# Attention with 16 queries a head: K loaded in 64 KB rows through a ring of two transposed pieces

## The chip, the cores and the metric

One Trainium2 chip, one core. The metric is device time in microseconds (us) of one execution, lower is better. The median of the runs shown is 631.35 us (3 runs, 631.29 to 631.35).

## The reference

```python
B, H, Sq, Skv, Dh = 8, 16, 16, 2048, 256        # all bfloat16
scale = q.shape[-1] ** -0.5
scores = jnp.einsum('bhqd,bhkd->bhqk', q, k) * scale
attn = softmax(scores, axis=-1)
return jnp.einsum('bhqk,bhkd->bhqd', attn, v)
```

There are 128 heads (8 batches of 16), each with only 16 queries against 2048 keys. K and V are 128 MiB each and each byte is used once, so nearly all that the kernel does is to move K and V from memory.

## The kernel before

**Blocks.** The 128 heads are taken eight at a time, in G = 16 blocks. A block's K is 8 MiB and so is its V. Each lies in SBUF with 128 tokens ("t") on every partition, 256 numbers a token, so a partition's share is one row of 64 KB in memory. A partition holds tokens of one head only: sixteen partitions make a head. `SL` has four slots of 64 tokens a partition: `VA, VB` hold a block's V, `KA, KB` its K.

**Score products (QK), lines 296 and 297.** K has the tokens on the partitions, and the product wants the head dimension there. DVE therefore transposes K in blocks of 32x32 words, in place in its slot (`kt`, line 200, 128x4096 words an instruction, four a block). The queries are laid out as sparse weights `QW`, which ACT writes for each block (`qwb`, line 256) from `QT`, a copy of Q that POOL makes at the start (line 184). PE then makes 64 products of 512 columns a block into the four banks of `S_ps`, one weight load for two products.

**Softmax.** DVE takes the row maximum over `S_ps` (line 222), ACT the exponential into `P_sb` with its row sum (line 282), DVE two transposes of `P_sb`, into `PTa` and `PTb` (lines 226 and 227), and the reciprocal.

**Weights' copies (`copies`, lines 207, 209 and 269).** The transposed probabilities are copied into the sparse weight tile `PTz`, in two halves e = 0, 1 for tokens 0 to 63 and 64 to 127. Each half takes eight copies, two for each quarter r of the partitions. DVE makes those of e = 0, r = 2, 3; ACT the other twelve.

**Output products (PV), line 317.** 128 products a block, each with its own weight load, 256 columns, summed in `O_ps`. PV needs all eight copies of e = 0 and the V of the block; from token 64 on the copies of e = 1. ACT then scales `O_ps` into `O_all` (`evac`, line 262); for the last block DVE does (line 247).

**Order.** The order on each engine is written out by hand, with semaphores between the engines. PE's loop runs QK of block r, then 20 spare products whose result is not used (`SPARE` = 5 rounds of four into `X_ps`), then PV of block r - 1. DVE's loop, for block g: maximum, two transposes of P, first transpose of the next K, its four copies, the other three transposes of K.

**Transfers.** All are issued by SP on one queue, in a fixed order: Q, K0, K1, V0, K2, V1, K3, V2 and so on. K goes in two transfers of 64 tokens a block (rows of 32 KB), V from block 2 on in one of 128 tokens (rows of 64 KB), V of blocks 0 and 1 in two of 64. A K transfer waits until PE has used that slot, a V transfer until PV of the block before has read V. At the end K15 goes in four transfers, V14 in three pieces, V15 in eight, the last of five tokens, so that PV can follow closely:

```python
PIECES = {last - 1: [(0, 60), (60, 39), (99, 29)],
          last: [(0, 28), (28, 32), (60, 23), (83, 16), (99, 11), (110, 8), (118, 5), (123, 5)]}
```

A piece (a, n) of V15 is issued when PV14 has read tokens up to a + n, rounded up to 16 tokens. Behind V15 go the output of fifteen blocks and, last, that of block 15.

Of the kernel before, what the change touches and what calls it, by code (L numbers as in the profile page):

```python
# [10 lines left out]
SP = mybir.EngineType.SP  # L11
BF16 = mybir.dt.bfloat16
# [3 lines left out]
SPARE = 5  # L16
VA, VB, KA, KB = 0, 1, 2, 3
# [3 lines left out]
def bass_standalone__softmax_full_bidir__sampling_kernel(  # L21
# [16 lines left out]
    ku = k.rearrange("b h s d -> (b h s) d").rearrange("(u p t) d -> u p t d", p=128, t=T)  # L38
# [4 lines left out]
    with ExitStack() as es:  # L43
        ec = es.enter_context
        SL = ec(nc.sbuf_tensor("SL", [128, 4, T, D], BF16))
        QT = ec(nc.sbuf_tensor("QT", [128, SQ * D], BF16))
        QW = ec(nc.sbuf_tensor("QW", [128, 2, 128, 8], BF16))

        P_sb = ec(nc.sbuf_tensor("P_sb", [128, 2080], BF16))

        PTa = ec(nc.sbuf_tensor("PTa", [128, T, 32], BF16))
# [5 lines left out]
        O_all = ec(nc.sbuf_tensor("O_all", [128, G + 2, D], BF16))  # L57
# [5 lines left out]
        O_ps = ec(nc.psum_tensor("O_ps", [128, 512], F32))  # L63
        X_ps = ec(nc.psum_tensor("X_ps", [128, 512], F32))

        def sem(name):
# [3 lines left out]
        s_k0 = [sem("s_k0a"), sem("s_k0b")]  # L70
        s_k = [sem("s_ka"), sem("s_kb")]
        s_kl = [sem("s_kla"), sem("s_klb")]
        s_v = sem("s_v")
        s_v0 = sem("s_v0")
# [5 lines left out]
        c_k0 = sem("c_k0")  # L80
        c_kt = [sem("c_kt0"), sem("c_kt1")]
# [11 lines left out]
        SLf = SL[:].bitcast(F32)  # L93

        QX = PTz[:, 1, 0:SQ * D // 128, :].rearrange("p t m -> p (t m)")

        QXu = QX.rearrange("p (c u a y) -> p a u c y", u=8, a=4, y=2)

        QTu = QT[:].rearrange("p (c u y) -> p u c y", u=32, y=2)

        SLk = SL[:].rearrange("p s (c t) (b i q) -> p s c b q t i", t=16, i=32, q=2)


        PIECES = {last - 1: [(0, 60), (60, 39), (99, 29)],
                  last: [(0, 28), (28, 32), (60, 23), (83, 16), (99, 11), (110, 8), (118, 5), (123, 5)]}

        s_p = {a: sem("s_p%d" % a) for a in sorted({a for w in PIECES for a, n in PIECES[w][1:]})}
        VW = SL[:, VA:VB + 1, :, :].rearrange("p a t d -> p (a t) d")

# [10 lines left out]
        def qx(Q, a):  # L120

            return (QTu[32 * a:32 * a + 32, 8 * Q:8 * Q + 8, :, :].rearrange("p u c y -> p c u y"),
                    QXu[32 * Q:32 * Q + 32, a, :, :, :].rearrange("p u c y -> p c u y"))

        def load_k(eng, g, e, slot, t0, n, s):
            eng.dma_start(SL[:, slot, t0:t0 + n, :], ku[2 * g + e, :, t0:t0 + n, :]).then_inc(s, 16)  # L126

        def on_sync(eng):
            def load_v(w, a, n):

                eng.wait_ge(c_pv, 8 * w + (a + n + C - 1) // C)
                eng.dma_start(VW[:, a:a + n, :], vb[w, :, a:a + n, :]).then_inc(s_p[a] if a else s_v, 16)  # L132

            eng.dma_start(QX, qh).then_inc(s_q, 16)
            for g, s0, s in ((0, VA, s_k0), (1, KA, s_k)):
                for e in range(2):
                    load_k(eng, g, e, s0 + e, 0, T, s[e])

            for e in range(2):
                eng.wait_ge(c_qk, 4 * e + 4)  # L140
                eng.dma_start(VW[:, T * e:T * e + T, :], vb[0, :, T * e:T * e + T, :]).then_inc(s_v0 if e else s_v, 16)
            for e in range(2):
                eng.wait_ge(c_qk, 4 * e + 12)
                load_k(eng, 2, e, KA + e, 0, T, s_k[e])
            for e in range(2):
                eng.wait_ge(c_pv, 4 * e + 12)
                eng.dma_start(VW[:, T * e:T * e + T, :], vb[1, :, T * e:T * e + T, :]).then_inc(s_v0 if e else s_v, 16)
            with nc.Fori(3, last, engines=[SP], hint_back_edge=True) as j:
                for e in range(2):
                    eng.wait_ge(c_qk, 8 * j + 4 * e - 4)  # L150
                    load_k(eng, j, e, KA + e, 0, T, s_k[e])
                load_v(j - 1, 0, 2 * T)
            for e in range(2):
                eng.wait_ge(c_qk, 8 * last + 4 * e - 4)
                load_k(eng, last, e, KA + e, 0, T // 2, s_k[e])
                load_k(eng, last, e, KA + e, T // 2, T // 2, s_kl[e])
            for w in PIECES:
                for a, n in PIECES[w]:
                    load_v(w, a, n)
            eng.wait_ge(c_ev, G)  # L160
            eng.dma_start(oh[:, 0:last, :], O_all[:, 2:G + 1, :]).then_inc(s_st, 16)
            eng.wait_ge(c_ev, G + 1)
            eng.dma_start(oh[:, last, :], O_all[:, G + 1, :]).then_inc(s_st, 16)
            eng.wait_ge(s_st, 32)

        def on_gpsimd(eng):

            for x, n in ([(c_pv, 8)] + [(x, 1) for x in s_kl] +
                         [(s_p[a], 16 * G - 16 * sum(a in dict(PIECES[w]) for w in PIECES)) for a in s_p]):
                eng.sem_inc(x, n)  # L170
            eng.memset(QW[:].rearrange("p e m x -> p (e m x)").bitcast(F32), 0.0).then_inc(c_qt, 1)
# [3 lines left out]
            eng.memset(P_sb[:, 0:16], 0.0).then_inc(c_mk, 1)  # L175
            eng.memset(P_sb[:, 2064:2080], 0.0).then_inc(c_mk, 1)
            eng.wait_ge(c_mk, 3)
# [3 lines left out]
            for n in range(16):  # L181

                eng.wait_ge(c_cq if n else c_pool, max(n, 1))
                eng.tensor_copy(*qx(n // 4, n % 4)).then_inc(c_cq, 1)  # L184

            eng.wait_ge(c_qw, 4)
            eng.wait_ge(c_cq, 16)
            eng.wait_ge(c_mk, 7)
            eng.memset(zero[1], 0.0).then_inc(c_pool, 1)

        def on_vector(eng):
# [6 lines left out]
            def kt(e, h, slot, n=1, first=False):  # L198
                x = SLf[:, slot, 32 * h:32 * h + 32 * n, :].rearrange("p t i -> p (t i)")
                eng.transpose(x, x).then_inc(c_k0 if first else c_kt[e], n)  # L200
# [11 lines left out]
            for e in range(2):  # L212
                eng.wait_ge(s_k0[e], 16)
                for h in range(2):
                    kt(e, h, VA + e, 1, True)

            eng.wait_ge(s_k[0], 16)
            kt(0, 0, KA, 2)
            eng.wait_ge(c_pool, 2)
            with nc.Fori(0, G, engines=[DVE]) as g:  # L220
                eng.wait_ge(c_qk, 8 * g + 8)
                eng.tensor_reduce(out=negm[:], in_=S_ps[:].rearrange("p c n -> p (c n)"),  # L222
                                  axis=AX.X, op=ALU.max, negate=True).then_inc(c_mx, 1)
                eng.wait_ge(c_ex, g + 1)
                eng.wait_ge(c_co[1], 8 * g + 1)
                eng.transpose(fa[:, 0:2048], P_sb[:, 16:2064]).then_inc(c_pt, 1)  # L226
                eng.transpose(fb[:, 0:2080], P_sb[:, 0:2080]).then_inc(c_pt, 1)  # L227
                eng.reciprocal(rinv[:, bass.ds(g + 2, 1)], lsum[:]).then_inc(c_ri, 1)
                mid = eng.to_reg((g + 15) & 15)
                with eng.If_lt(mid, 14):  # L230
                    eng.wait_ge(s_k[0], 16 * g + 16)
                    kt(0, 0, KA)
                eng.wait_ge(c_pt, 2 * g + 2)
                eng.wait_ge(c_pv, 8 * g + 4)
                copies(0, (2, 3))
                with eng.If_lt(mid, 14):
                    eng.wait_ge(s_kl[0], ((g + 2) & 16) + 1)
                    kt(0, 1, KA)
                gg = eng.to_reg(g)
                with eng.If_lt(gg, last):  # L240
                    eng.wait_ge(s_k[1], 16 * g + 16)
                    kt(1, 0, KB)
                    eng.wait_ge(s_kl[1], ((g + 2) & 16) + 1)
                    kt(1, 1, KB)
            eng.wait_ge(c_pv, 8 * G + 8)
            eng.wait_ge(c_ri, G + 1)
            eng.tensor_scalar(out=O_all[:, G + 1, :], in0=O_ps[:, 0:D], scalar1=rinv[:, G + 1:G + 2],  # L247
                              scalar2=None, op0=ALU.mult).then_inc(c_ev, 1)

        def on_scalar(eng):  # L250
            def qwb(src):
                for a in range(4):
                    dv = QW[32 * a:32 * a + 32, :, 16 * a:16 * a + 64, :]
                    dv = bass.AP(tensor=dv.tensor, offset=QW[32 * a:32 * a + 32, 0, 16 * a, :].offset,
                                 ap=[list(dv.ap[0]), [1024 + 512, 2], [2, 64], [1, 2]])
                    eng.activation(dv, src(a), ACTF.Copy, scale=scale).then_inc(c_qw, 1)  # L256

            def evac(n):

                eng.wait_ge(c_pv, 8 * n)  # L260
                eng.wait_ge(c_ri, n)
                eng.activation(O_all[:, bass.ds(n, 1), :].rearrange("p o d -> p (o d)"), O_ps[:, 0:D], ACTF.Copy,  # L262
                               scale=rinv[:, bass.ds(n, 1)]).then_inc(c_ev, 1)
# [7 lines left out]
            for x in (c_ev, c_ri, c_co[1]):  # L271
                eng.sem_inc(x, 1)
# [19 lines left out]
        def on_tensor(eng):  # L292
# [31 lines left out]
            for c in range(4):  # L324
                if c == 0:
                    eng.wait_ge(c_pool, 1)
# [69 lines left out]
```

## Time and profile before

| | |
|---|---|
| median of the runs | 631.35 us |
| the profiled execution, first to last instruction | 630.1 us |
| outside that span (median less span) | 1.25 us |
| DMA queue | 270.54 MB, busy 99.9% of 16 engines' span, 429 GB/s |
| PE matmul, DVE, ACT, POOL busy | 85%, 67%, 43%, 4% |
| mean granted TensorE clock | 0.976 |

The page gives the profiled execution alone, and its own time is that of its span; the runs' times are taken without a profile and hold what lies around the span. A wait's row names what ended it. The chain that ended last is followed back from the last instruction: it tells what released each step, not whether the step had room.

### The profile page before, as it was taken

How to read it: one execution, taken by the hardware profiler on the slowest of the kernel's cores; microseconds unless marked ns; L12 is line 12 of the kernel's file. 1: busy time of each engine (PE TensorE's matmuls, PEld its weight loads, DVE VectorE, ACT ScalarE, POOL GpSimd, SP SyncE). 2: the span in 40 equal slices, each digit the busy share in tenths (PEclk: the TensorE clock that was granted, in tenths of full speed). 3: DMA queues.
4: the chain of work that ended last, by engine and by line, in shares of the span. 5: the costliest groups of instructions: out<-in, count | busy, mean ns of one | idle time of the engine just before them, and what ended most of it. 6: DMA issues, size and time to landing. Idle time of an engine off the chain costs nothing.

```text
span 630.1 us, 7710 instructions
## 1 busy us (share of the span) xinstructions
PE 535.6 (85%) x3336; PEld 273.4 (43%) x2561; DVE 419.4 (67%) x193; ACT 269.1 (43%) x308; POOL 26.0 (4%) x30
## 2 busy tenths in 40 slices
PE   1658989889888898888978889888889878899997
PEld 0112734518244272542726336263362724518386
DVE  1989694865849657496574956749566594768740
ACT  1016562723437243362534525335263352732653
POOL 7800000000000000000000000000000000000000
PEclk9998989999899998999999899999998999999999
DMA  9999999999999999999999999999999999999999
GB/s 377 433 435 431 433 431 424 433 439 426 466 399 466 408 433 441 424 441 424 437 453 408 458 408 458 416 424 441 424 441 449 408 458 408 458 404 421 435 428 376
DMA packets 11008, 270.54 MB, mean 429 GB/s; under 512 B 1024, under 2 KB 3072, under 8 KB 3584
## 3 DMA queue, kind: packets, MB, share of 16 engines
q1 hardware_dynamic: 11008, 270.54, 99.9%
HBM read 269.48 MB, written 1.05 MB: 429 GB/s over the span
## 4 chain that ended last, share of the span: by engine, by line
DMA 57%; PE 34%; issue 4%; DVE 4%; SPq 0%; DVEq 0%; ACT 0%
DMA SL<-in_v_dram 52%; PE O_ps L317 30%; DMA SL<-in_k_dram 5%; DVE SL L200 2%; PE S_ps L296 1%; PE S_ps L297 1%; DVE PTb L227 1%; DVE negm L222 1%; PE X_ps L297 1%; SPq L132 0%; DVE PTz L207 0%; DVE PTz L209 0%; SPq L126 0%; ACT P_sb L282 0%; DVE O_all L247 0%
## 5 line engine op out<-in xcount | busy, mean ns | idle before, releaser
L200 DVE STREAM_TRANSPOSE SL<-SL 128x4096 f32<-128x4096 f32 (+1 forms) x63 | 280.6, 4492 | 88.1 <-DMA SL<-in_k_dram 87.6
L296 PE MATMUL S_ps<-SL,QW 128*128 128x512 bf16 (+1 forms) x512 | 206.1, 403 | 57.6 <-DVE SL L200 48.9
L317 PEld LDWEIGHTS O_ps<-SL,PTz 128*128 128x128 bf16 x2048 | 198.9, 98 | 114.2 <-issue 89.0
L317 PE MATMUL O_ps<-SL,PTz 128*128 128x256 bf16 x2048 | 226.6, 273 | 24.9 <-DMA SL<-in_v_dram 23.8
L297 PE MATMUL S_ps<-SL,QW 128*128 128x512 bf16 (+1 forms) x512 | 205.6, 401 | 0.0
L296 PEld LDWEIGHTS S_ps<-SL,QW 128*128 128x128 bf16 (+1 forms) x512 | 74.4, 145 | 230.1 <-issue 161.9
L256 ACT ACTIVATE QW<-QT 32x256 bf16 x64 | 26.9, 420 | 168.5 <-PE S_ps L297 167.3
L269 ACT ACTIVATE PTz<-PTa 16x1024 bf16<-16x1024 bf16 x32 | 33.8, 1056 | 128.9 <-PE O_ps L317 114.2
L222 DVE TENSOR_REDUCE negm<-S_ps 128x1 f32<-128x2048 f32 x16 | 36.6, 2289 | 58.3 <-PE S_ps L297 58.3
L269 ACT ACTIVATE PTz<-PTa,mk 32x1024 bf16<-32x1024 bf16 x64 | 72.3, 1130 | 0.0
L269 ACT ACTIVATE PTz<-PTb 16x1024 bf16<-16x1024 bf16 x64 | 67.2, 1051 | 1.2
L226 DVE STREAM_TRANSPOSE PTa<-P_sb 128x2048 bf16<-128x2048 bf16 x16 | 37.0, 2312 | 35.4 <-ACT P_sb L282 35.4
L297 PE MATMUL X_ps<-QT,QW 128*128 128x512 bf16 x260 | 58.2, 379 | 0.0
L227 DVE STREAM_TRANSPOSE PTb<-P_sb 128x2080 bf16<-128x2080 bf16 x16 | 36.8, 2302 | 0.0
L269 ACT ACTIVATE PTz<-PTb,mk 32x1024 bf16<-32x1024 bf16 x32 | 36.2, 1132 | 0.0
L282 ACT ACTIVATE P_sb<-S_ps,negm 128x2048 bf16<-128x2048 f32 x16 | 31.5, 1967 | 5.9 <-DVE negm L222 5.9
L262 ACT ACTIVATE O_all<-O_ps,rinv 128x256 f32 x15 | 7.1, 473 | 39.8 <-PE O_ps L317 39.8
L184 POOL COPY QT<-PTz 32x1024 bf16<-32x1024 bf16 x16 | 17.4, 1087 | 2.4 <-DVE PTz L194 1.5
L207 DVE TENSOR_SCALAR PTz<-PTb,mk 32x1024 bf16<-32x1024 bf16 x32 | 15.2, 476 | 0.0
L209 DVE COPY PTz<-PTa 16x1024 bf16<-16x1024 bf16 x32 | 13.5, 422 | 1.1
L247 DVE TENSOR_SCALAR O_all<-O_ps,rinv 128x256 bf16<-128x256 f32 x1 | 0.5, 484 | 20.4 <-PE O_ps L317 20.4
L296 PE MATMUL S_ps<-PTz 128*128 128x512 bf16 x1 | 0.6, 608 | 9.9 <-ACT QW L256 9.9
(18 smaller groups left out, 21.0 us busy)
## 6 DMA issues: line engine op xcount, KB each, us to landing
SL<-in_k_dram SPq DMA_DIRECT2D x30, 4096.0 KB, 24.2
SL<-in_v_dram SPq DMA_DIRECT2D x4, 4096.0 KB, 21.3
SL<-in_k_dram SPq DMA_DIRECT2D x4, 2048.0 KB, 21.5
SL<-in_v_dram SPq DMA_DIRECT2D x1, 3840.0 KB, 21.3
SL<-in_v_dram SPq DMA_DIRECT2D x1, 2496.0 KB, 22.0
SL<-in_v_dram SPq DMA_DIRECT2D x1, 2048.0 KB, 12.2
SL<-in_v_dram SPq DMA_DIRECT2D x1, 1856.0 KB, 24.7
SL<-in_v_dram SPq DMA_DIRECT2D x1, 1792.0 KB, 10.8
```

What stands on the lines that cost most here:

```text
L184: eng.tensor_copy(*qx(n // 4, n % 4)).then_inc(c_cq, 1)
L200: eng.transpose(x, x).then_inc(c_k0 if first else c_kt[e], n)
L207: ins = eng.tensor_scalar(out=dst, in0=src, scalar1=m, scalar2=None, op0=ALU.mult)
L222: eng.tensor_reduce(out=negm[:], in_=S_ps[:].rearrange("p c n -> p (c n)"), axis=AX.X, op=ALU.max, negate=True).then_inc(c_mx, 1)
L226: eng.transpose(fa[:, 0:2048], P_sb[:, 16:2064]).then_inc(c_pt, 1)
L227: eng.transpose(fb[:, 0:2080], P_sb[:, 0:2080]).then_inc(c_pt, 1)
L256: eng.activation(dv, src(a), ACTF.Copy, scale=scale).then_inc(c_qw, 1)
L269: eng.activation(dst, src, ACTF.Copy, scale=m if x else 1.0).then_inc(c_co[e], 1)
L282: eng.activation(P_sb[:, 16:2064], sv, ACTF.Exp, bias=negm[:], scale=1.0, accum_out=lsum[:]).then_inc(c_ex, 1)
L296: return eng.matmul(dst, w, x, start=start, stop=stop, skip_group_check=not check)
L297: return eng.add_instruction(mybir.InstMatmult(name=nc.get_next_instruction_name(), engine=PE, start_tensor_calc=start, stop_tensor_calc=stop,
L317: ins = eng.matmul(O_ps[:, 0:D], PTz[:, t // T, t % T, :], VW[:, t, :], start=(t == 0), stop=(t == 2 * T - 1))
```

## The change

- K comes as one transfer of 128 tokens a block (blocks 2 to 14), in rows of 64 KB. K0, K1 and K15 come in three transfers, of 56, 32 and 40 tokens. V of blocks 0 and 1 comes in one transfer each, V15 in seven pieces.
- K is no longer transposed in place. DVE transposes it in eight pieces of N = 16 tokens, alternately into two places of a ring (`RING`), and PE makes 16 products of 256 columns, each with its own weight load, from a piece. Piece i (from 2 on) waits for PE's products of piece i - 2.
- POOL copies (moves) the first MV = 24 tokens of each block's K to a place behind it, `KM`. The pieces are read in the order 24 to 127, then the moved 0 to 23, so that the last piece and a half lie outside the place that the next transfer overwrites. K's next transfer waits for the move (`c_x`) and for the first half of piece 6 (`c_ks`).
- V's tokens lie 24 places on, cyclically, in the two V slots.
- `P_sb` is laid into the ring's first place, and Q's copy into the space of the output tile (`OQ`), so `QT` and `O_all` go. Its zero edges are set by DVE in each block.
- `O_ps` has two banks, used in turn.
- Copies: DVE makes e = 0, r = 1, 2, 3 and e = 1, r = 3; ACT e = 0, r = 0 and e = 1, r = 0, 1, 2.
- Order on DVE: softmax of block h - 1, then all transposes of K of block h, then the copies of block h - 1. On ACT the exponential comes before `qwb`. On PE: QK of block r, PV of block r - 1, then 28 spare products (7 rounds, blocks 1 to 13). Ahead of QK of block 0 there are 8 spare products, ahead of block 1 24.
- `QW` has its weights in contiguous columns.

```diff
-SPARE = 5
+MV = 24
+N = 16
+SPARE = 7
...
-        SL = ec(nc.sbuf_tensor("SL", [128, 4, T, D], BF16))
+        SL = ec(nc.sbuf_tensor("SL", [128, 4 * T + MV + 2 * N, D], BF16))
...
+        VW, KW = SL[:, 0:2 * T, :], SL[:, 2 * T:4 * T, :]
+        KM = SL[:, 4 * T:4 * T + MV, :]
+        KP = SL[:, 2 * T + MV:4 * T + MV, :]
+        RING = [SL[:, 4 * T + MV + i * N:4 * T + MV + (i + 1) * N, :] for i in range(2)]
+        P_sb = SL[:, 4 * T + MV:4 * T + MV + N, :].rearrange("p t d -> p (t d)")[:, 0:2080]
+        PIECES = {last - 1: [(0, 60), (60, 44), (104, 24)],
+                  last: [(0, 28), (28, 32), (60, 25), (85, 19), (104, 11), (115, 8), (123, 5)]}
...
 on_sync
+            parts = [(0, MV + 2 * N, s_k), (MV + 2 * N, 2 * N, s_kb), (MV + 4 * N, 40, s_kc)]
+            load_k3(0, [])
+            eng.wait_ge(c_x, 1)
+            load_k3(1, [(c_kt, 2), (c_kt, 4), (c_ks, 1)])
+            load_v(0, 0, 2 * T)
+            with nc.Fori(2, last, engines=[SP], hint_back_edge=True) as j:
+                eng.wait_ge(c_ks, j)
+                eng.wait_ge(c_x, j)
+                load_k(eng, j, KW, 0, 2 * T, s_k)
                 load_v(j - 1, 0, 2 * T)
...
 on_gpsimd
+            def move(n):
+                eng.wait_ge(s_k, 16 * n + 16)
+                eng.sem_inc(c_mk, 1)
+                eng.tensor_copy(KM.rearrange("p t d -> p (t d)"),
+                                KW[:, 0:MV, :].rearrange("p t d -> p (t d)")).then_inc(c_x, 1)
...
+            with nc.Fori(1, G, engines=[POOL]) as n:
+                eng.wait_ge(c_kt, 8 * n)
+                move(n)
...
 on_vector
+            def kt(i, a, n, s):
+                eng.transpose(words(RING[i % 2][:, a:a + n, :]), words(KP[:, N * i + a:N * i + a + n, :])).then_inc(s, 1)
...
+            with nc.Fori(0, G + 1, engines=[DVE]) as h:
+                with eng.If_ne(hh, 0):
...
+                    eng.memset(edge, 0.0)
                     (maximum, P's two transposes, reciprocal, of block h - 1)
+                with eng.If_lt(hh, G):
+                    eng.wait_ge(s_k, h16)
+                    for i in range(8):
...
+                        if i > 1:
+                            eng.wait_ge(c_qk, 8 * h + i - 1)
+                        if i == 6:
+                            kt(i, 0, N // 2, c_ks)
+                            eng.wait_ge(c_x, h + 1)
+                            kt(i, N // 2, N // 2, c_kt)
+                        else:
+                            kt(i, 0, N, c_kt)
+                with eng.If_ne(hh, 0):
+                    eng.wait_ge(c_pool, 2)
+                    eng.wait_ge(c_pv, 8 * g + 4)
+                    copies(0, (1, 2, 3))
+                    eng.wait_ge(c_pv, 8 * h)
+                    copies(1, (3,))
...
 on_tensor
+            with nc.Fori(0, G + 1, engines=[PE], hint_back_edge=True) as r:
+                for i, n, w, c in ((0, 2, c_pv, 8), (1, 6, c_ex, 1)):
+                    with eng.If_eq(rr, i):
+                        with nc.Fori(0, n, engines=[PE]) as x:
+                            eng.wait_ge(w, c)
+                            spare(OQ[:, 0, 0:128], OQ[:, 0:2, :], True)
                 with eng.If_lt(rr, G):
+                    eng.wait_ge(c_qw, 4 * r + 4)
+                    with nc.Fori(0, 4, engines=[PE]) as j:
+                        for i in range(2):
+                            eng.wait_ge(c_kt, w)
+                            qk(S_ps[:, bass.ds(j, 1), 256 * i:256 * i + 256].rearrange("p o n -> p (o n)"),
+                               split(RING[i])).then_inc(c_qk, 1)
+                with eng.If_ne(rr, 0):
+                    eng.wait_ge(c_ev, rr)
+                    eng.wait_ge(c_co[0], 8 * r)
+                    eng.wait_ge(s_v, r16)
+                    pv(r, (w15, w14), O_ps[:, bass.ds(r & 1, 1), 0:D].rearrange("p o d -> p (o d)"))
+                    with eng.If_lt(mid, last - 2):
+                        with nc.Fori(0, SPARE, engines=[PE]) as x:
+                            eng.wait_ge(c_qw, 4 * r + 8)
+                            spare(QW[:, 1, 7, :], QW[:, 0, 0:4, :], False)
```

More of the change, by code (lines that the diff above doesn't have):

```diff
@@ L11 @@
 SP = mybir.EngineType.SP
+POOL = mybir.EngineType.Pool
 BF16 = mybir.dt.bfloat16
@@ L44, in bass_standalone__softmax_full_bidir__sampling_kernel @@
         ec = es.enter_context
-        SL = ec(nc.sbuf_tensor("SL", [128, 4, T, D], BF16))
[L46 to L51, printed above, removed]
+        SL = ec(nc.sbuf_tensor("SL", [128, 4 * T + MV + 2 * N, D], BF16))
+        QW = ec(nc.sbuf_tensor("QW", [128, 2, 8, 128], BF16))
+        OP = ec(nc.sbuf_tensor("OP", [128, last * D + T * 32], BF16))
         PTb = ec(nc.sbuf_tensor("PTb", [128, T + 1, 32], BF16))
@@ L55, in bass_standalone__softmax_full_bidir__sampling_kernel @@
         mk = ec(nc.sbuf_tensor("mk", [128, 1], F32))
-        O_all = ec(nc.sbuf_tensor("O_all", [128, G + 2, D], BF16))
+        OQ = OP[:, 0:G * D].rearrange("p (g d) -> p g d", d=D)
+        PTa = OP[:, last * D:].rearrange("p (t x) -> p t x", x=32)
         negm = ec(nc.sbuf_tensor("negm", [128, 1], F32))
@@ L134, in on_sync @@
             eng.dma_start(QX, qh).then_inc(s_q, 16)
[L135 to L151, printed above, removed]
+            parts = [(0, MV + 2 * N, s_k), (MV + 2 * N, 2 * N, s_kb), (MV + 4 * N, 40, s_kc)]
@@ L152, in on_sync @@
                 load_v(j - 1, 0, 2 * T)
[L153 to L156, printed above, removed]
+            eng.wait_ge(c_ks, last)
+            eng.wait_ge(c_x, last)
+            load_k3(last, [])
             for w in PIECES:
@@ L174, in on_gpsimd @@
             eng.memset(mk[:], 1.0).then_inc(c_mk, 1)
[L175 to L177 removed]
+            eng.wait_ge(c_mk, 1)
             for r in range(4):
@@ L210, in copies @@
                         ins.then_inc(c_co[e], 1)
[L212 to L244, printed above, removed]
@@ L245, in on_vector @@
             eng.wait_ge(c_pv, 8 * G + 8)
             eng.wait_ge(c_ri, G + 1)
-            eng.tensor_scalar(out=O_all[:, G + 1, :], in0=O_ps[:, 0:D], scalar1=rinv[:, G + 1:G + 2],
+            eng.tensor_scalar(out=OQ[:, last, :], in0=O_ps[:, 0, 0:D], scalar1=rinv[:, G + 1:G + 2],
                               scalar2=None, op0=ALU.mult).then_inc(c_ev, 1)
@@ L289, in on_scalar @@
                     evac(g + 1)
-                copies(1, (0, 1, 2, 3))
+                copies(1, (0, 1, 2))
         def on_tensor(eng):
```

191 lines of the change are left out of this document (101 added, 90 removed).

## The prediction

> **What bounds the kernel now.** I read the page's head and queue, then the chain in order of time, then one steady block and the end in the timeline.
>
> ```profile
> span 630.1 us, 7710 instructions
> PE 535.6 (85%) x3336; PEld 273.4 (43%) x2561; DVE 419.4 (67%) x193; ACT 269.1 (43%) x308; POOL 26.0 (4%) x30
> PEclk9998989999899998999999899999998999999999
> q1 hardware_dynamic: 11008, 270.54, 99.9%
> ```
>
> The one queue has packets under way for 99.9% of the span; no engine comes near. So time can only come from what the queue spends beside the bytes, and can be lost wherever it runs empty or work is left behind its last byte.
>
> ```profile
> 219.24 0.23 issue
> ...
> 233.78 24.24 DMA SL<-in_v_dram
> 258.02 0.23 issue
> ...
> 568.23 0.23 issue
> ...
> 627.21 0.05 issue
> 627.26 0.73 PE O_ps L317 x5
> ```
>
> Each "issue" row starts where a V transfer has landed. From 219.24 to 258.02, 38.78 us, the queue moved 256 tokens in three transfers. From V13's landing (568.23) to V15's (627.21), 58.98 us, it moved 384 tokens in fifteen (K15 4, V14 3, V15 8). One and a half steady blocks would be 58.17 us with 4.5 transfers, so 0.81 us lies on 10.5: **0.077 us a transfer**, and (38.78 - 0.23) / 256 = 0.1506 us a token. A V in one transfer takes 19.35 us. The chain names PE's products before each V; but V is issued at 233.78 and the queue holds K until 219.24 + 19.43 = 238.67, so nothing waits there. At the end PE is done 0.8 us after the last V.
>
> **Fewer transfers.** Before, K takes 34 transfers and V 27; after, K 3 + 3 + 13 + 3 = 22 and V 14 + 3 + 7 = 24. Fifteen fewer at 0.077 give **-1.15 us** if the queue stays full: the last V lands at 626.06. Up to V13 it is thirteen fewer, 1.00 us: V13 lands at 567.23, K14 at 547.88. The Trainium skill, page "SBUF — State Buffer", section "The DMA setup-cost knee", puts a roughly fixed 2 us on every transfer and advises the largest single one; by that the fifteen would be worth 30 us. The rows above say 0.077, since the next transfer is already queued, so I take that.
>
> **Work of a block, after.** The durations:
>
> ```profile
> 217.81 2.31 DVE L226 STREAM_TRANSPOSE PTa<-P_sb 128x2048 bf16<-128x2048 bf16 x1 [2.21 <-ACT P_sb L282]
> 219.47 14.13 PE L317 MATMUL O_ps<-SL,PTz 128*128 128x256 bf16 x128 [1.88 <-DMA SL<-in_v_dram]
> 220.05 2.30 DVE L227 STREAM_TRANSPOSE PTb<-P_sb 128x2080 bf16<-128x2080 bf16 x1
> ...
> 228.97 4.45 DVE L200 STREAM_TRANSPOSE SL<-SL 128x4096 f32<-128x4096 f32 x1 [6.58 <-DMA SL<-in_k_dram]
> ...
> 233.45 0.42 DVE L209 COPY PTz<-PTa 16x1024 bf16<-16x1024 bf16 x1
> 233.47 0.43 PEld L296 LDWEIGHTS S_ps<-SL,QW 128*128 128x128 bf16 x2 [0.15 <-DVE SL L200]
> ...
> 235.16 13.10 DVE L200 STREAM_TRANSPOSE SL<-SL 128x4096 f32<-128x4096 f32 x3
> ...
> 251.94 4.48 PE L297 MATMUL X_ps<-QT,QW 128*128 128x512 bf16 x20
> ...
> 261.10 0.12 DVE L228 RECIPROCAL rinv<-lsum 128x1 f32 x1
> ```
> ```profile
> L317 PE MATMUL O_ps<-SL,PTz 128*128 128x256 bf16 x2048 | 226.6, 273 | 24.9 <-DMA SL<-in_v_dram 23.8
> ...
> L194 DVE STREAM_TRANSPOSE PTz<-PTz 128x2048 f32<-128x2048 f32 x1 | 2.3, 2311 | 5.8 <-DMA PTz<-in_q_dram 5.8
> ```
>
> - A piece of K is 128x2048 words: 2.31 us, and 2.24 from start to start (217.81 to 220.05). Piece 6 in halves I take at 0.15 more: 128x4096 takes 13.10 / 3 = 4.37, so a second start costs about 0.1 to 0.15.
> - A 256-column product with its own load takes (14.13 - 0.27) / 127 = 0.109 (L317: one takes 0.27), PV 13.97, a piece's sixteen 1.75, its last one ending 1.91 after its first starts.
> - PE starts after a wait: 0.05 at 233.47 (load, after 228.97 + 4.45), 0.23 at 219.47. The new waits go through registers, so I take 0.23.
> - A pair of copies on DVE: (235.16 - 233.45) / 2 = 0.855; three pairs 2.57.
> - A spare product is (4.48 - 0.38) / 19 = 0.216; 28 are 6.04.
>
> Pieces 2 to 7 wait for PE two pieces back: 2.31 + 0.23 + 1.91 + 0.04 = 4.49 for two, 2.245 each, and DVE alone needs 2.24. So **six pieces are 13.62 us**.
>
> New in the order is a circle through PE and DVE: spares 6.04, piece 0's products 1.95, six pieces 13.62, copies 2.57, PE's start 0.23, PV 13.97. Sum **38.4 us**; the queue's block becomes 38.70. So the queue stays the bound, with 0.3 us to spare a block. From K's landing: piece 0 is ready after 2.33, PE starts at 2.56, piece 2 at 4.51, copies end at 20.70, PV runs from 20.93 to 34.9, the next V is issued at about 35.2. The queue empties at 38.70; the last store lands 1.55 us after its issue (628.53, row below, to the span's end at 630.08), so 2 us are left. K's next transfer, after piece 6's first half, is issued near 16 of 19.35: the same holds.
>
> ```profile
> 28.19 0.38 PE L297 MATMUL S_ps<-SL,QW 128*128 x1
> 28.92 0.44 PE L296 MATMUL S_ps<-SL,QW 128*128 x1 [0.35 <-issue]
> ```
>
> QK becomes a loop of four turns, with a turn before pieces 2, 4 and 6. The trace's loop on PE that waits in each turn loses 0.73 - 0.22 = 0.51 us a turn. A piece leaves PE 2.245 - 1.75 = 0.50 us, so I take 0.04 a turn; the bounds are 0 and 0.51.
>
> **POOL's move** is 128x6144, from the landing of K's first part, beside the first pieces on DVE.
>
> ```profile
> L184 POOL COPY QT<-PTz 32x1024 bf16<-32x1024 bf16 x16 | 17.4, 1087 | 2.4 <-DVE PTz L194 1.5
> L189 POOL MEMSET PTz<- 128x4096 f32 x1 | 3.5, 3520 | 0.1
> ```
>
> At L184's 1.06 ns a number it takes 6.5 us, at the fill's rate for words (3072 of them) 2.6. I take 6.5, nothing on the path: it must be done 15 us after K's landing (piece 6), in the first block 9 (Q lands at 5.8 by L194's wait, K0's first 56 tokens 8.5 later at 14.3, all of K0 at 25.3, and K1 must be issued 1.55 before that). Twice 6.5 costs nothing later and 3.6 us in the first block.
>
> **Start.** From K0's last landing, 25.3, four pieces and the last products take 11.3: 36.6. Softmax takes 9.3 us (from QK's end at 251.94 to 261.22): 45.9, if POOL's second fill is done before the exponential (14.3 + 6.5 + 12 copies of 1.09 + 3.5 = 37.4; it is). K1's pieces to the half of 6 take 14.8: K2 is issued at 60.7, and V0 empties the queue at 5.8 + 58.4 = 64.2. Cost 0, cover 2 us. The spare products ahead of blocks 0 and 1 fill waits for K and for the exponential: 0, and at worst 5.2 us (24 of 0.216) less that cover.
>
> **The end** loses its cover. Before, QK15 ran on pieces transposed early; after, DVE transposes K15 only behind block 14's softmax, piece 2 only behind PV13, and its copies for PV14 behind all eight.
>
> ```profile
> 597.15 14.13 PE L317 MATMUL O_ps<-SL,PTz 128*128 128x256 bf16 x128 [0.45 <-DMA SL<-in_v_dram]
> ...
> 611.83 1.04 ACT L269 ACTIVATE PTz<-PTb 16x1024 bf16<-16x1024 bf16 x1
> ...
> 628.53 0.35 SPq L163 DMA_DIRECT2D out_dram<-O_all  x1
> ```
>
> In steps: K14 lands 547.88; PV13 starts 20.93 later, 568.80, not at 567.4 when V13 is there, and leaves PE at 582.77. Piece 0 of K15 is ready; its products end 584.68; six pieces to 598.34; copies to 600.91; PV14 from 601.14 (before: 597.15) to 615.11. V15's first piece is issued 32 products into PV14, at 604.9, and V14's last lands at 567.23 + 39.02 = 606.25: 1.35 ahead, so the queue may stand 0.2 us here, which PE's lag hides. PV15 needs ACT's six copies for e = 1: PV14's last product ends at 615.27, the first copy starts 0.55 later (611.83 against 597.15 + 14.13), six at about 1.05 take 6.3, so with PE's start they are there at 622.35, against 622.09 when PE reaches token 64: 0.26 lost. PV15's last product ends at 615.11 + 0.26 + 13.86 + 0.27 = **629.50**, 3.4 us behind the last V (626.06). Before, PE waited for the last V and ended at 628.0. Then DVE 0.5, SP 0.05, store 1.55: **631.6**, with six loop turns of 0.04 (blocks 14 and 15) 631.8. That is +1.75 against 630.08 (628.53 + 1.55). This execution's 630.1 stands 1.25 below the median, so on the median it is **633.1 us**.
>
> So the fifteen transfers save 1.15 us that the end does not show, and PV14, starting 4 us later, turns PV15 from waiting for V into what V's end waits for.
>
> **Rivals.**
>
> *The transfers set the end after all.* Then it is 631.35 - 1.15 = 630.2. PV15's end would have to come 2.9 us sooner, so the twelve pieces on the end's path (two times six) would have to go at 2.0 us each, not 2.24: a transpose from one place into another that is faster than one in place. Against it: from P_sb to PTa takes 2.31, the same as in place (L194). For it: there is no row for 32-bit words into another place.
>
> *The circle becomes longer than the queue's block.* Place: PE's loop turns between pieces, or the spares' rounds, which now wait. It decides from 0.3 us a block, 0.1 a turn over the 0.50 that is hidden. At 0.25 a turn the circle is 39.15: 0.45 over in 13 blocks, 5.9 less 2 of cover, and 1.5 + 2 more at the end: near 640. The row bounds an exposed turn by 0 and 0.51; 0.25 is the middle. 634 to 641.
>
> *POOL's move is slow,* over 9 us: the queue runs empty once near 25 us. 633.5 to 636.
>
> *The clock falls.* The PEclk row of the head has an 8 in several of its 40 slices of 15.75 us: each lost 1.6 to 3.2 us of full speed. In the new order PE is idle only 0.5 us at a time, so I expect no more of it. One such loss inside the last two blocks' products costs just that: 634.7 to 636.3.
>
> *Each transfer holds the queue for 2 us, and fifteen of them go:* 631.35 - 30 = 601; the queue's 99.9% and the 0.077 speak against it. (This is the rule of the Trainium skill's page above.)
>
> **Numbers.** End bound by PE as summed: 0.52, with its own range 632.2 to 634.6. Transfers set the end: 0.17. Longer circle: 0.19. Slow move: 0.06. Clock: 0.05. The 2 us rule: 0.01. The range takes in 630.2 and most of the longer circle: 629.9 to 637.5, leaving out the circle's upper half, part of the slow clock and the rule. A measurement of this kernel tells 0.2%, 1.26 us, from no change: below 630.09 is faster, above 632.61 slower. Faster: half of the second case and the rule, 0.10. Same: the other half and 0.13 of the first, 0.22. Slower: 0.68.
>
> **What the profile after would show.** V landing every 38.70 us in steady blocks and queue share near 99.5%; 46 loads; DVE pieces 2.24 apart; PV13 starting some 1.5 us after V13's landing; PV14 near 601; no wait of PV15 for V after its start; the last V some 3 us ahead of PE's end. Wrong if V's landings are over 38.8 apart (circle), if PV15 waits for its last piece (transfers), or if a gap stands near 25 us in the queue (move).

## The result: 641.0 us, slower by 1.5%

The changed kernel takes 641.0 us (median of five runs, 639.1 to 643.2); the kernel before takes 631.35. The ratio is 1.0155, with a 95% interval from 1.0137 to 1.0173. 633.1 was predicted, with a range of 629.9 to 637.5. The profiled execution of after has a span of 639.7 us where 631.8 was forecast, so 7.9 us are to be explained.

The page of after, the lines that answer to those of before:

```profile
span 639.7 us, 11266 instructions
PE 563.6 (88%) x4492; PEld 387.2 (61%) x4104; DVE 451.4 (71%) x354; ACT 257.4 (40%) x240; POOL 109.2 (17%) x44
PEclk9889999999999999999999999999999999999999
q1 hardware_dynamic: 8848, 270.54, 99.1%
```

The bytes are the same, the packets fewer (8848 against 11008), no engine is at its limit, and PE's clock is better than before. But the queue's share is 99.1% and not 99.9%. Next the chain in order of time, K's transfers of four steady blocks (start, duration, what; the start is the issue on SP, the end is the landing that DVE waited for):

```profile
177.93 24.19 DMA SL<-in_k_dram
...
216.83 23.99 DMA SL<-in_k_dram
...
255.54 25.22 DMA SL<-in_k_dram
...
295.46 24.23 DMA SL<-in_k_dram
```

Start plus duration gives K's landings: 202.12, 240.82, 280.76 and 319.69. The blocks are 38.70, 39.94 and 38.93 us long. The first is what the prediction had; the others are longer, by amounts that differ. The timeline of the 39.94 block:

```profile
222.76 14.14 PE L350 MATMUL O_ps<-SL,PTz 128*128 128x256 bf16 x128 [0.72 <-DVE PTz L227]
...
237.08 0.33 SPq L139 DMA_DIRECT2D SL<-in_v_dram  x1
...
240.84 17.83 DVE L220 STREAM_TRANSPOSE SL<-SL 128x2048 f32<-128x2048 f32 x9 [8.03 <-DMA SL<-in_k_dram]
...
261.74 0.50 PE L350 MATMUL O_ps<-SL,PTz 128*128 128x256 bf16 x3 [0.99 <-DMA SL<-in_v_dram]
```

DVE stood idle for 8.03 us until K landed, so the engines are not late as a whole. V5 is issued at 237.08, 3.74 us before K's landing at 240.82; that is the **lead**, and it will be used in this sense: from a transfer's issue to the last landing of the transfer ahead of it. V5 then landed at 261.41, 20.6 us after K and not 19.35: 1.23 us lost, at this one boundary. One of its first packets, begun at 239.9, took 4.26 us; 64 KB packets take 2.42 otherwise.

Adding up the boundaries of after from V0's landing (63.96) to V13's (573.54): 509.58 us for 26 transfers of 19.35, so 6.5 us are lost. K2 lost 1.45 with a lead of 2.0, V1 0.62 with 2.6, K3 0.29 with 4.6; of the twelve later V, with leads of 3.7 to 4.7, seven lost between 0.16 and 1.2 and five nothing to speak of; the other K, with 4.6 to 5.9, lost nothing. In the kernel before V has 4.9 us, as its rows in the prediction show (issued at 233.78, the queue full until 238.67), K 6 to 15, and nothing is lost.

After V13's landing before needs 61.9 us (568.23 to 630.1), after 66.2 (573.54 to 639.7). Last rows of after's timeline:

```profile
607.39 14.14 PE L350 MATMUL O_ps<-SL,PTz 128*128 128x256 bf16 x128 [0.71 <-DVE PTz L227]
611.09 11.77 SPq L139 DMA_DIRECT2D SL<-in_v_dram  x7
...
622.31 14.15 PE L350 MATMUL O_ps<-SL,PTz 128*128 128x256 bf16 x128 [0.77 <-issue]
622.90 0.44 SPq L166 DMA_DIRECT2D out_dram<-OP  x1
636.50 0.48 DVE L274 TENSOR_SCALAR OP<-O_ps,rinv 128x256 bf16<-128x256 f32 x1 [14.09 <-PE O_ps L350]
637.01 0.35 SPq L168 DMA_DIRECT2D out_dram<-OP  x1
```

PV14 starts at 607.39 behind DVE's copies, PV15 0.77 us after PV14's end, and waits for no V; PE sets the end, as forecast. The last store is issued at 637.01 and lands 2.6 us later, not 1.55.

So the theory is that **a transfer issued too late before the queue runs dry costs time although it is issued before that**, and that the 1.55 us of cover in the prediction was the wrong price. Its rivals: POOL's move, which runs when K has just landed; K's 64 KB rows; a clock or a wait of PE that goes with V's boundary alone.

### The profile page after: what moved, and what is told of

Same layout as the page of the kernel before. It is cut to its first block, busy times and chain, and to the rows that moved or that the text cites. A ratio compares the mean times of both kernels' runs of the same rounds, so it can differ in the third digit from the quotient of the medians.

```text
span 639.7 us, 11266 instructions
## 1 busy us (share of the span) xinstructions
PE 563.6 (88%) x4492; PEld 387.2 (61%) x4104; DVE 451.4 (71%) x354; ACT 257.4 (40%) x240; POOL 109.2 (17%) x44
## 3 DMA queue, kind: packets, MB, share of 16 engines
q1 hardware_dynamic: 8848, 270.54, 99.1%
## 4 chain that ended last, share of the span: by engine, by line
DMA 53%; DVE 20%; issue 17%; PE 9%; SPq 0%; DVEq 0%; ACT 0%; ACTq 0%
DMA SL<-in_k_dram 53%; DVE SL L220 19%; PE O_ps L350 7%; PE S_ps L326 1%; PE X_ps L327 1%; SPq L132 0%; DVE PTb L243 0%; DVE negm L238 0%; DVE PTz L227 0%; DVEq L259 0%; DVE PTz L229 0%; DVE OP L274 0%; SPq L141 0%; DVEq L232 0%; ACT SL L309 0%
## 5 line engine op out<-in xcount | busy, mean ns | idle before, releaser
L220 DVE STREAM_TRANSPOSE SL<-SL 128x2048 f32<-128x2048 f32 (+1 forms) x144 | 285.9, 2050 | 119.4 <-DMA SL<-in_k_dram 115.8
L326 PEld LDWEIGHTS S_ps<-SL,QW 128*128 128x128 bf16 x2048 | 187.2, 96 | 187.2 <-issue 160.0
L326 PE MATMUL S_ps<-SL,QW 128*128 128x256 bf16 x2048 | 248.3, 272 | 45.0 <-DVE SL L220 44.8
L184 POOL COPY SL<-SL 128x6144 bf16<-128x6144 bf16 x16 | 84.9, 5308 | 474.2 <-DMA SL<-in_k_dram 474.2
L309 ACT ACTIVATE SL<-S_ps,negm 128x2048 bf16<-128x2048 f32 x16 | 31.5, 1967 | 323.1 <-DVE negm L238 323.1
L327 PE MATMUL X_ps<-QW 128*128 128x512 bf16 x364 | 80.7, 379 | 0.0
L283 ACT ACTIVATE QW<-OP 32x256 bf16 x60 | 80.2, 1336 | 1.1
L242 DVE STREAM_TRANSPOSE OP<-SL 128x2048 bf16<-128x2048 bf16 x16 | 37.0, 2312 | 38.1 <-ACT SL L309 38.1
L298 ACT ACTIVATE PTz<-OP,mk 32x1024 bf16<-32x1024 bf16 x48 | 54.2, 1130 | 0.0
L243 DVE STREAM_TRANSPOSE PTb<-SL 128x2080 bf16<-128x2080 bf16 x16 | 36.8, 2302 | 0.0
L298 ACT ACTIVATE PTz<-OP 16x1024 bf16<-16x1024 bf16 x16 | 16.9, 1055 | 5.3 <-DVE PTb L243 4.9
## 6 DMA issues: line engine op xcount, KB each, us to landing
SL<-in_k_dram SPq DMA_DIRECT2D x3, 3584.0 KB, 13.3
```

Source lines behind the costliest of these rows:

```text
L184: eng.tensor_copy(KM.rearrange("p t d -> p (t d)"), KW[:, 0:MV, :].rearrange("p t d -> p (t d)")).then_inc(c_x, 1)
L220: eng.transpose(words(RING[i % 2][:, a:a + n, :]), words(KP[:, N * i + a:N * i + a + n, :])).then_inc(s, 1)
L283: eng.activation(dv, src(a).rearrange("p e (q b) y -> p e q b y", b=4), ACTF.Copy, scale=scale).then_inc(c_qw, 1)
L298: eng.activation(dst, src, ACTF.Copy, scale=m if x else 1.0).then_inc(c_co[e], 1)
L309: eng.activation(P_sb[:, 16:2064], sv, ACTF.Exp, bias=negm[:], scale=1.0, accum_out=lsum[:]).then_inc(c_ex, 1)
L326: return eng.matmul(dst, w, x, start=start, stop=stop, skip_group_check=not check)
```

## Experiments

**V later, in the kernel before.** It has neither move nor ring nor 64 KB rows of K. SP makes empty loop turns (3 or 6) between its wait for PE and V's issue:

```diff
 eng.wait_ge(c_pv, 8 * w + (a + n + C - 1) // C)
+eng.sem_inc(c_sp, 1)
+with nc.Fori(0, 3, engines=[SP]) as x:
+    eng.wait_ge(c_pv, 8)
 eng.dma_start(VW[:, a:a + n, :], ...)
```

> The kernel before, with V's transfer of blocks 2 to 13 issued about 1.2 us later (three empty loop turns on SP behind its wait for the products of V); nothing else is changed. There V is issued 4.9 us before the transfers ahead of it end, and the queue loses nothing; here it would be issued some 3.7 us before. Theory (late issue): a transfer issued less than about 4 us before the queue's end starts late, as in the changed kernel, where leads of 3.7 to 4.7 us cost 0.2 to 1.2 us at about every second V: 0.2 to 0.5 us a block here, 634 to 637 us. Rival 1 (the cover is the 1.55 us that the last store took, as the prediction had it): no loss, 631.4. Rival 2 (what slows the queue is K's 64 KB rows or POOL's move, neither of which is in this kernel): no loss, 631.4.

> The same with six empty turns, about 2.3 us, so that V is issued some 2.6 us before the transfers ahead of it end. Late issue: 0.6 to 1.4 us a block over twelve blocks, 638 to 648 us. A cover of 1.55 us: no loss, 631.4. 64 KB rows of K or POOL's move: no loss, 631.4. If what counts is the number of packets still to go and not the time, the 32 KB rows of K in this kernel need half the lead: no loss in the run with three turns, and some loss here, 632 to 636.

Measured: 640.2 us (1.0132, 1.0107 to 1.0157) and 654.8 us (1.0361, 1.0338 to 1.0385). The rivals that need the move or K's rows fall, and so does a cover of 1.55 us. Both are slower than I expected, and the chains in order of time show why, first of three turns, then of six:

```profile
142.64 15.81 PE O_ps L322 x128
...
356.82 23.13 DMA SL<-in_v_dram
379.95 0.23 issue
380.19 14.15 PE O_ps L322 x128
```
```profile
367.52 21.79 DMA SL<-in_v_dram
389.31 0.29 issue
389.60 16.50 PE O_ps L322 x128
```

With three turns the lead is 3.5 to 4.0 in eight blocks (some lose nothing, some 0.3 to 0.9), but 2.1 to 2.4 in four, and three of these lose 1.3 to 2.9 us. These four stand behind a PV of 15.5 to 15.8 us, like the one at 142.64, where it takes 14.15 otherwise. PE had waited 2.2 to 4.7 us for V ahead of them, and 1.9 ahead of most others; its granted clock was 0.91 from 142 to 160 us and 1.00 from 379 to 396. So PE, after a longer wait, mostly works at a lower clock, though not each time: the PV at 224.34 had waited 3.2 us and took 14.15. With six turns every PV from block 2 to block 13 takes 16.5 to 16.9 us, behind waits of 3.2 to 4.5 (the profiled execution, 660.2 us, is the slowest of four; its mean clock is 0.929, before's 0.976). A slower PV makes the next V later still, and the lead settles near 0.25 us, with 2.1 to 2.6 us lost per block. So the delay feeds itself; the leads below are therefore always read from the trace and not from the edit.

**V earlier, in the changed kernel, in two ways.** One splits V of blocks 1 to 13, so that its first part needs 112 of PE's products and not 128. The other takes three pairs of copies from DVE's path (block 15 excepted):

```diff
-load_v(j - 1, 0, 2 * T)
+for a, n in [(0, 104), (104, 24)]:
+    load_v(j - 1, a, n)
```
```diff
 (DVE)
-eng.wait_ge(c_pv, 8 * g + 4)
-copies(0, (1, 2, 3))
+with eng.If_eq(hh, G):
+    eng.wait_ge(c_pv, 8 * g + 4)
+    copies(0, (1, 2, 3))
 (ACT)
 copies(0, (0,))
+with eng.If_ne(gg, last):
+    copies(0, (1, 2, 3))
```

> The changed kernel, with V of blocks 1 to 13 in two transfers of 104 and 24 tokens, so that the first is issued when PE is done with 112 tokens and not with 128: 1.75 us earlier, some 5.5 us before K's end. Late issue: the losses behind K from V1 on go (0.6 at V1, 0.2 at V2 and V3, some 3.9 us after that), thirteen more transfers cost 1.0: V13 lands near 570.0 and not 573.5, and the time is 637 to 638.5. 64 KB rows of K or POOL's move as the cause: the losses stay, and 1.0 us comes on top, 642.

> The changed kernel, with the three pairs of copies of the first half's weights for the blocks up to 14 made by ACT and not by DVE (block 15's stay on DVE). They stand on the way from K to V's issue with 2.6 us, so V is issued 2.6 us earlier, some 6.3 us before K's end; and PV14 at the end starts 2.6 us earlier. Late issue: V's losses go, V13 lands near 569.2; with an end that is 2.6 to 3.3 us shorter the time is 633 to 634.5. 64 KB rows of K or POOL's move as the cause of the losses: V13 stays at 573.5 and only the end gains, 637.5 to 638.5.

Measured: 636.9 us (1.0095, 1.0078 to 1.0112), V13 at 568.4; and 634.3 us (1.0051, 1.0034 to 1.0068), V13 at 568.65. Both undo V's losses, all but 0.3 to 0.5 at V1, with the move and K's 64 KB rows still in place. That V13 came 1.6 us sooner than expected with V in two parts is chance at K2, which the edit does not touch: there it had a lead of 3.1 and lost nothing. The copies' kernel shows the boundary sharply: V's lead became 4.6 and not the 6.3 I expected (PV now waits for PE's own last scores instead of the copies, and gains 0.9 us, not 2.6), and that was enough. Its chain from block 3 on is a ruler:

```profile
370.52 23.97 DMA SL<-in_k_dram
...
409.21 23.99 DMA SL<-in_k_dram
...
447.92 23.97 DMA SL<-in_k_dram
```

K lands at 394.49, 433.20, 471.89: 38.70 us a block, no loss, on either boundary.

**The rivals by themselves.** POOL's move made twice (the copy and its wait doubled in `move`, from block 1 on); and K of blocks 2 to 14 in two transfers of 32 KB rows:

```diff
-load_k(eng, j, KW, 0, 2 * T, s_k)
+load_k(eng, j, KW, 0, T, s_k)
+load_k(eng, j, KW, T, T, s_kb)
```

> The changed kernel with POOL's move made twice in every block from the second on, 10.6 us and not 5.3 from K's landing; it is needed only some 15 us after the landing. Late issue: nothing hangs on it, the leads stay, 638 to 642 us. If POOL's traffic at the time of the boundary slows the transfers, the losses grow by about as much again: 645 to 648.

> The changed kernel with K of blocks 2 to 14 in two transfers of 64 tokens (32 KB rows, as before the change), while DVE and POOL wait for both halves as they waited for the whole: V is issued as long after K's landing as in the changed kernel, 3.7 us before the queue's end, but behind 32 KB packets. Late issue, counted in time: V still loses at some of the boundaries; K's second half gives the next K nothing, thirteen more transfers cost 1.0 us: 638 to 643. If K's 64 KB rows are the cause, or the number of packets still to go, V's losses go: 635 to 637.

Measured: 640.2 us (1.0148, 1.0133 to 1.0164) and 643.7 us (1.0205, 1.0185 to 1.0225). The doubled move, in the timeline:

```profile
201.60 5.31 POOL L186 COPY SL<-SL 128x6144 bf16<-128x6144 bf16 x1 [28.18 <-DMA SL<-in_k_dram]
207.08 5.31 POOL L190 COPY SL<-SL 128x6144 bf16<-128x6144 bf16 x1 [0.17 <-POOL SL L186]
```

Twice the copying from K's landing on, and the queue lost 4.9 us up to V13 where after lost 6.5: nothing added (the difference is K2, which had a lead of 2.9 and lost nothing). The second copy comes only behind the boundary's first packets; that the first one is not the cause either is shown by the kernels above, which lose without a move and, with the copies on ACT, lose nothing with it. With 32 KB rows of K, the lead of V is 3.5 to 4.8 from V2 on, about as in after, and V still loses up to 1.3 us at a boundary (6.0 up to V13 in all). K3's first half, itself in 32 KB rows, lost 0.4 with a lead of 3.9. What counts is the time, not the size of the packets that are still to go.

**K2 earlier.** On top of the copies on ACT, K2 in three transfers:

```diff
+load_k3(2, [(c_kt, 10), (c_kt, 12), (c_ks, 2)])
+load_v(1, 0, 2 * T)
-with nc.Fori(2, last, engines=[SP], hint_back_edge=True) as j:
+with nc.Fori(3, last, engines=[SP], hint_back_edge=True) as j:
```

> The changed kernel with the copies on ACT as before, and K2 in three transfers like K1, so that its first is issued when two of K1's pieces are transposed and not when seven and a half are: some 12 us earlier, well over 10 us before V0's end and not 2.9. Late issue: the 1.0 us that the queue lost at K2 and the 0.5 at V1 go, two more transfers cost 0.15: V13 lands near 567.3 and not 568.65, the time is 632.9. If what is lost in the first blocks belongs to the first blocks (the moves, the first softmax, the clock) and not to the lead, V13 stays near 568.7 and the time at 634.3.

Measured in the trace: K2's first issue at 50.65, lead 13.3, nothing lost at K2; V1 has a lead of 3.3 and loses 0.3; V13 lands at 567.47, 1.2 sooner, as expected to 0.2. The time does not follow: 634.2 us (1.0046, 1.0032 to 1.0060), against 634.3 and the 632.9 expected. The spans of all runs show half of it (median 632.3 against 632.9), and 1.4 to 1.9 us lay outside them, against 1.3 to 1.7. The profiled execution was the fastest of the five, 633.4; what the others lost is not in a trace, and stays open.

**K later, with PE's order untouched.** The kernel with the copies on ACT, where both leads are 4.6; SP makes 1, 3 or 6 empty turns ahead of K's issue of blocks 2 to 14, in the manner of the first experiment.

> The kernel with the first half's copies on ACT, in which K and V are both issued 4.6 us before the queue's end and nothing is lost from block 3 on. Here K's issue of blocks 2 to 14 is put off by one empty loop turn on SP, 0.4 to 0.6 us, so that its lead is some 4.1 us; PE, DVE and the order of the work are as they were. Late issue: a little is lost at some of the K boundaries, 0 to 0.4 us each, 635 to 638. If only V's boundary can lose, because PE waits there and its clock falls, nothing is lost: 634.3.

> The same with three turns, about 1.2 us: K's lead is some 3.4 us. Late issue: about 0.5 us at each K, 638 to 642. Only V's boundary: 634.3.

> The same with six turns, about 2.3 us: K's lead is some 2.3 us. Late issue: 1.0 to 1.5 us at each K, 647 to 654. Only V's boundary: 634.3. If the cover were the 1.55 us of the prediction: 634.3 too.

Measured: 633.9 us (1.0043, 1.0026 to 1.0060), 645.5 us (1.0216, 1.0199 to 1.0233) and 651.7 us (1.0333, 1.0305 to 1.0362). The chains in order of time, one turn, three, six:

```profile
215.45 23.64 DMA SL<-in_k_dram
...
254.14 23.64 DMA SL<-in_k_dram
```
```profile
139.98 23.23 DMA SL<-in_k_dram
...
179.04 23.63 DMA SL<-in_k_dram
...
219.85 24.27 DMA SL<-in_k_dram
```
```profile
182.37 21.81 DMA SL<-in_k_dram
...
221.07 23.54 DMA SL<-in_k_dram
...
263.07 22.07 DMA SL<-in_k_dram
```

One turn leaves K a lead of 4.3: from block 4 on every block is 38.7 (239.09 to 277.78), nothing is lost, where 0 to 0.4 a block was expected, and the time is that of 4.6. Three turns leave 3.5: K lands at 163.21, 202.67 and 244.12, blocks of 39.46 and 41.45. Six leave 2.4 to 2.7 in eight blocks and less in five: K lands at 204.18, 244.61 and 285.14. The first of these blocks, of 40.43, had a lead of 2.45 and lost 1.7 (the block before, at the same lead, lost nothing, so it is a matter of chance); the second, of 40.53, had only 0.9, for the reason that follows. V, nearly always with 4.6 or more, loses little in all three. So it is no matter of V's boundary; the time of K's own issue is enough. The 41.45 block shows the feedback again: PE had waited 2.0 us for K's first piece, its granted clock was 0.91 from 202 to 222 and 1.00 in the windows beside it, and the next K was issued at 219.85, with a lead of 2.2.

**All boundaries together.** From all fourteen traces, before's and after's included, the transfers of K and V issued between 60 and 575 us; lost is the time between landings beyond that of the bytes:

| lead, us | boundaries | over 0.1 us lost | mean loss, us |
|---|---|---|---|
| under 0.5 | 12 | 12 | 2.33 |
| 0.5 to 1.5 | 5 | 5 | 1.80 |
| 1.5 to 2.5 | 18 | 14 | 1.27 |
| 2.5 to 3.5 | 13 | 8 | 0.43 |
| 3.5 to 3.9 | 34 | 24 | 0.52 |
| 3.9 to 4.3 | 19 | 9 | 0.20 |
| 4.3 to 4.6 | 26 | 2 | 0.02 |
| over 4.6 | 337 | 12 | 0.01 |

Even at 3.5 to 3.9 us, more than twice the 1.55 of the prediction, seven in ten lost something. A second reason is in the traces: the sixteen DMA engines finish a transfer 0.3 to 3 us apart, and a loss on one of them widens this, so that the first of them runs dry sooner the next time. By the lead to the first engine's end the mean losses sort more evenly: 0.64 us at 1.5 to 2.5, 0.14 at 2.5 to 3.0, 0.03 at 3.0 to 3.5, 0.005 over that. Why the first packets of a transfer are slow when it comes late is not settled by these runs.

**The end.** Two kernels on top of K2 in three: K15's pieces transposed in place, so that DVE need not wait for PE; the second one has the copies in equal halves on ACT and DVE instead of the branch for block 15.

```diff
 (DVE, block 15)
+with eng.If_eq(hh, last):
+    ...
+    x = words(KP[:, N * i:N * i + N, :])
+    eng.transpose(x, x).then_inc(c_kt, 1)
 (the second kernel)
-copies(0, (1, 2, 3))   # DVE
+copies(0, (2, 3))
-copies(0, (0,))        # ACT
+copies(0, (0, 1))
```

> The kernel with K2 in three transfers, and in the last block K15's pieces transposed in place instead of through the ring of two, so that DVE need not wait for PE between them, and PE's last scores don't wait for DVE. Theory (PE sets the end, through the ring's pace in block 15): PV14 starts some 2 us earlier, 30.2 us after V13's landing; PV15 then ends just behind the last V, the end after V13 is 62.5 us and not 64.3, and the time is 631.1, the same as before the change. If something else sets the end (the last V, the output's store), PV14 starts earlier and the time stays at 632.9.

> The changed kernel with K2 in three transfers, K15's pieces in place, and the first half's weights copied by ACT for two groups of rows and by DVE for two, in every block (so no branch for the last block). V should be issued 0.8 us earlier after K's landing than in the changed kernel, some 4.5 us before K's end, and K2 over 10 us before V0's end. Late issue: V13 lands at 567.5, PV14 starts 30.3 us later, PV15 ends just behind the last V, the span is 629.5 to 630 and the time 630.8 to 631.4: the change's whole loss is back. If V's third piece of the last block is late again as in the run with the pieces in place (4.8 us for 25 tokens, where 3.9 is what they take), because what delays it is not that run's extra branch, the time is 632 to 633.

Measured: 633.3 us (1.0028, 1.0017 to 1.0038) and 633.6 us (1.0035, 1.0023 to 1.0047). The ends of the chains, of the copies on ACT, of the first and of the second kernel:

```profile
600.85 13.97 PE O_ps L354 x128
614.82 0.77 issue
615.59 14.16 PE O_ps L354 x128
```
```profile
599.71 10.49 PE O_ps L368 x96
610.20 0.02 issue
610.22 12.12 DMA SL<-in_v_dram
622.34 0.05 issue
622.38 2.90 PE O_ps L368 x25
```
```profile
615.11 9.45 PE O_ps L364 x85
624.56 0.03 issue
624.59 4.88 PE O_ps L364 x43
```

With the copies on ACT PE sets the end, 64.3 us after V13. With the pieces in place PV14's first product starts 30.3 us after V13, in the second kernel 30.4 (with the copies on ACT alone 32.0), and PV15 waits for V again, as in the kernel before, though in the second kernel only 0.3 us; the end is 63.0 and, in the second kernel, 62.5 us after V13. So the ring's pace in block 15 had cost 1.3 to 1.8 us of the end; the 0.6 to 1.1 us that still stand against before's 61.9 were not followed further. Neither time shows the gain in full, and both missed what was expected (631.1, and 630.8 to 631.4): in the profiled executions V13 landed at 569.3 and 569.6, not 567.5. Of that 1.3 to 1.4 us has the reason given in the last section, and the rest was lost at the boundaries from V1 on. No version beat the kernel before. It could hardly: V13 at 567.2 is 1.0 us sooner than before, and that is all the fewer transfers hold.

## Why the prediction was wrong, step by step

**The step that failed is the cover.** The prediction wrote "the queue empties at 38.70; the last store lands 1.55 us after its issue ..., so 2 us are left", and for K "near 16 of 19.35; the same holds", and "Start ... Cost 0, cover 2 us". The issue times came near: V was issued 34.96 us after K's landing (forecast 35.2), K 14.7 (near 16), K2 at 61.96 (60.7), V0's landing at 63.96 (64.2). So V had 3.7 us where the forecast gave it 3.5, and K2 had 2.0 where it gave 3.5; both were called enough as forecast. K was to have 3.4 and had 4.6 or more, so that K lost almost nothing is luck: "near 16" was a slip beside the prediction's own 14.8 for the same pieces in its Start. The price was taken from one small store at an emptying queue, where the question was how long ahead a full queue needs the next transfer. The nearest row to that was V's own 4.9 us in the kernel before, and it bounded the answer only from above; below it the trace had nothing, and the range should have been open there. The term was 0; it measured 6.3 us, V13 landing at 573.54 and not at 567.23.

A page of the Trainium skill, "SBUF — State Buffer", section "The DMA setup-cost knee", speaks of a roughly fixed 2 us a transfer, mostly completion. As the time that a lead must cover it would have been too short as well: at 1.5 to 2.5 us 14 of 18 boundaries lost something. As a price for each transfer it is refuted here as the prediction said: with the losses gone but for 0.3 us in each, K2 in three and V in two parts differ by eleven transfers up to V13, and by 0.9 us (V13 at 567.47 and 568.37), 0.08 each.

**The end** was forecast 64.6 us after V13, and took 66.2; the rest of the error. PV13 started 1.3 us after V13 (forecast 1.57), PV14 33.85 (33.91): the circle through DVE and the ring was right to a tenth in sum. Then PE lost 0.77 us between PV14 and PV15, in which the trace shows register steps at the loop's turn, behind its branches, and no product; no copy of ACT's was waited for, which had been given 0.26. V15's first piece had a lead of 1.4, called "may stand 0.2 us"; the piece landed 1.0 late, all of V15 2.7, the 960 KB of output behind it, and the last store, 64 KB, behind that: 2.6 us and not 1.55.

**Right:** 0.077 us a transfer; 2.24 us a piece (PE's pieces start 2.19 to 2.29 apart), a turn of PE's loop hidden in the pieces; the move, 5.31 us where 6.5 was taken, and nothing on the path, even twice; PE's clock no worse.

**The rivals.** "The circle becomes longer than the queue's block" had 634 to 641, "near 640", the number that came out, but not its mechanism: DVE waits 8 us for K in each block, and PE is done with the spares before the first piece. Its sign, V's landings over 38.8 apart, was a poor one, since a queue that stands gives the same; the idle time ahead of DVE's first piece tells the two apart. The transfers did not set the end, the move was not slow, the clock did not fall.

## What to carry to other kernels

Where one queue is the bound, look up for each transfer how long before the queue's end it is issued, and treat the smallest lead that the trace shows without a loss as the price, not the time that some idle transfer takes: here 4.3 us kept the queue full, 3.7 did not. A change that moves work ahead of an issue is costed against that lead, and a few tenths of a microsecond on that path can be worth nothing or 0.5 us a block. A loss there can feed itself, through an engine that waits, slows and issues the next one later.

## What the runs showed that was not expected

**A fetch of instructions can shift the whole kernel.** Both kernels with the extra code for K15 had a packet of another queue near 16 us, in the middle of K0; none of the other twelve traces has one between 1 and 600 us. The queues from 10 to 20 us in the last kernel, then DVE's first pieces there and in the kernel with K2 in three:

```profile
q1 hardware_dynamic: 254, 4.42, 103.1%
q8 instruction: 1, 0.02, 0.6%
```
```profile
20.38 4.50 DVE L223 STREAM_TRANSPOSE SL<-SL 128x2048 f32<-128x2048 f32 x2 [1.89 <-DMA SL<-in_k_dram]
```
```profile
19.11 4.50 DVE L223 STREAM_TRANSPOSE SL<-SL 128x2048 f32<-128x2048 f32 x2 [0.50 <-DMA SL<-in_k_dram]
```

The packet (16 KB, 0.95 us) held one of the sixteen engines: fifteen of them ended K0's second part by 18.85, as without it, the last at 20.25. A transfer lands with its last engine, so this one landed 1.3 us later, and V0 at 65.2 and not 63.9: the queue never makes it up. The Trainium skill, page "Runtime: NRT & Kernel Launch", section "Instruction fetch mechanics", calls the cost of such a refill of 16 KB mostly hidden. For the data on a queue that is never empty it was not. Smaller ones, of 8 KB, came 12 to 15 us before the end in the six kernels with a branch for block 15's copies and in no other; in the first kernel with the pieces in place, where two of them fell there, V15's third piece took 4.8 us, and in the second one, without that branch, 3.8. That these packets come with the code is argued from where they appear; it was not tried alone.

**ACT pays for scattered writes.** The four small copies that lay out Q's weights now write single numbers 128 apart, and before pairs of neighbours; their groups on the page, before and after:

```profile
L256 ACT ACTIVATE QW<-QT 32x256 bf16 x64 | 26.9, 420 | 168.5 <-PE S_ps L297 167.3
```
```profile
L283 ACT ACTIVATE QW<-OP 32x256 bf16 x60 | 80.2, 1336 | 1.1
```

0.42 us against 1.34 for the same 32x256, off the path here. The source is read in pairs of neighbours in both, so the writes are the likely reason; they were not changed alone.
